# A decode kernel (attention, output projection and gated MLP): TensorE's program in two loops of two rounds, and wide matmuls for half of the output weights

## The chip, the cores and the metric

The kernel runs on one core of one Trainium2 chip. The time is device microseconds from the start of the execution to its end, lower is better. The time line of the profile is some 1.7 us shorter, because it runs from the first instruction to the last.

## The reference, cut to what matters

```python
# x: (4, 1, 512).  32 query heads, 8 heads in the cache, head size 128, all bfloat16
# k_cache, v_cache: (4, 8, 4096, 128); only the last W = 1024 rows count
xn = layernorm(x)
q = xn @ wq                                  # wq: 512 x 4096
p = softmax(q @ k.T * 128 ** -0.5)           # k, v: last 1024 rows, each head for 4 query heads
s = (p @ v) @ wo                             # wo: 4096 x 512
h = gelu(layernorm(xn) @ w1 + b1)            # w1: 512 x 1792
g = silu(h @ w2 + b2)                        # w2: 1792 x 512
return x + s * g
```

With four rows of x there is little arithmetic; nearly all of the work is to read 8 MB of K, 8 MB of V, 4 MB each of wq and wo, and 1.75 MB each of w1 and w2.

## The kernel before

Every operation is recorded in a list for its engine, with the operations that it depends on, and the program is then written out in full. The SyncE queue issues the large loads in a fixed order. The parts that matter here (cuts are marked); PV(g) multiplies the softmax weights of head g by its rows of V:

```python
def load_k(g):                 # 1 MB a head; eight buffers of 1 MB, V takes those of K
    d_k[g] = pg.dma("sp", "k%d" % g, lambda e: e.dma_start(
        kv_buf[:, g, :, :].rearrange("p c d -> p (c d)"), cache_rows(A_k_cache, g)))
# ...
d_wq = [load_wq(0)]
load_k(0)
load_k(1)
d_wq.append(load_wq(1))
for g in range(2, HKV):
    load_k(g)
# ... transposes T(n) and scores S(n): 32 units of 8 tiles, written out
for n in range(LAG, NUN + LAG):
    if n < NUN:
        T(n)
    S(n - LAG)
load_v(0); ...w1...; load_v(1); ...w2...
for g in range(HKV):
    if g >= 2:
        load_v(g)
    if g == 4:                 # 128 rows of wo, scattered over few DMA engines
        R3 = (7 * 512 + 384) * D
        d_wox = [pg.dma("sp", "wox%d" % h, lambda e, h=h: e.dma_start(
            wox_sb[32 * h:32 * h + 12, 0:5, :].rearrange("p j o -> p (j o)"),
            bass.AP(A_wo.tensor, R3 + 60 * h * D, [[5 * D, 3], [15 * D, 4], [1, 5 * D]])),
            t_q) for h in range(2)]
        d_wox.append(...)      # the last 8 rows
    PV(g)
    # ... epilogue of the head before; mlp1 after head 0, mlp2 and mlp3 after head 1
# ...
def wo(tiles, *deps):          # the narrow form: weights are loaded, 4 columns stream
    def fn(pe):
        for w, o, st, sp in tiles:
            for c in range(4):
                last = pe.matmul(psM[:, PS_W + c * 4:PS_W + (c + 1) * 4],
                                 w[:, c * 128:(c + 1) * 128], o,
                                 start=(st and c == 0), stop=sp, skip_group_check=True)
        return last
    return add("pe", fn, *deps)

rows = to_rows()               # after head 7: attention output to rows, as wo is laid out
wo([...scattered rows: 24 matmuls...], rows[2], mlp["g"], *d_wox)
for g0, g1, i0, i1, d in d_wo:         # pieces of wo: 2 + 2 + 2 + 1 heads
    wo([(wo_sb[:, g, i, :], OW[:, i, g * 4:(g + 1) * 4], False, False)
        for g in range(g0, g1) for i in range(i0, i1)], d, rows[0], mlp["g"])
for i0, i1, d in d_w3:                 # last head: 256 rows, then 128
    t_w = wo([(wo_sb[:, 7, i, :], OW3[:, i * 4:(i + 1) * 4], False, i == 2)
              for i in range(i0, i1)], d, rows[1])
# multiply by g, transpose, add x, store
```

The narrow form of wo has the output's 512 columns in four pieces on the partitions of PSUM, and so ends in the layout that the last multiplication wants.

The softmax here doesn't subtract the row's maximum and nothing guards it: scores larger than these inputs give would overflow.

## Time and profile before

| kernel before | value |
|---|---|
| time, median of three runs | 76.72 us (76.69 to 76.80) |
| span in the profile | 75.0 us |
| bytes read | 28.85 MB |
| TensorE instructions written, by the prediction's count | 2204 (1089 matmuls with their weight loads; the trace has 2202 records) |
| last landing of wo (semaphore records) | 71.89 us |
| end of the last wo matmul | 72.2 us |

The page counts 16 DMA engines for the core, and a load of 128 KB or more has 16 landing records on its semaphore (the last piece of wo in before: 70.25 to 71.89 us). Each is taken here as one engine delivering its share. The kernel's waits are for the last of them.

The prediction below shows the page's slices, the chain of waits and the time line. In a group the columns are line, engine, operation, output and inputs, shapes (the weights' rows and columns with a star, then what streams), count, then busy time in us and mean ns of one, then the idle time before and what ended most of it.

```profile
DMA 39%; PE 34%; SPq 15%; DVE 5%; issue 3%
...
L555 PE MATMUL psM<-OW,wo_sb 128*128 128x4 bf16 x124 | 4.1, 167 | 0.8 <-DMA wo_sb<-in_A_wo_dram 0.8
...
L555 PEld LDWEIGHTS psM<-OW,wo_sb 128*128 128x128 bf16 x124 | 3.7, 105 | 1.1 <-DMA wo_sb<-in_A_wo_dram 0.9
```

The narrow matmuls of wo wait 0.8 us for wo's loads. Records overlap: 64 of these matmuls took 1.87 us in the time line, 0.029 us for each, though one record is 167 ns long. So what a group costs is read from the time line, not from its mean.

### The profile page before, as it was taken

Reading aid. Unit: us, or ns where it says so; the run is one execution under the profiler, and the core shown is the slowest. Engines: PE = TensorE matmul, PEld = TensorE weight load, DVE = VectorE, ACT = ScalarE, POOL = GpSimd, SP = SyncE. Lnnn points to the kernel's source line nnn. Section 1 sums busy time; section 2 is a strip of 40 time slices with the busy share of each in tenths; the row PEclk is TensorE's granted clock in tenths of the full one; section 3 lists DMA queues with packets and bytes.
Section 4 is the critical chain, followed back from the end, with each engine's and each line's share of the span. In section 5 each row is a group of like instructions: output and inputs, shape, how many; then the busy total and the mean of one; then the engine's idle time right before and its main releaser. Section 6 shows DMA issues by size and latency. Waiting matters only on the chain.

```text
span 75.0 us, 2384 instructions
## 1 busy us (share of the span) xinstructions
PE 49.1 (66%) x1089; PEld 40.3 (54%) x1089; DVE 41.2 (55%) x84; ACT 9.7 (13%) x16; POOL 7.2 (10%) x19
## 2 busy tenths in 40 slices
PE   0000029965689999959979937910899977379670
PEld 0000029953279989959979902500886555268640
DVE  0778106894258989959977060269639774620020
ACT  0611000000270320303203600230000000000000
POOL 6999300000000000000000000000000000000000
PEclk9999999999999999999999995555555555555555
DMA  1999999998999999999999999999999999999800
GB/s 37 271 413 420 417 420 476 437 420 376 433 437 433 415 433 420 424 415 464 419 398 425 461 413 401 424 420 428 419 429 428 420 409 420 417 411 419 322 25 2
DMA packets 4266, 28.99 MB, mean 387 GB/s; under 512 B 508, under 2 KB 648, under 8 KB 1697
## 3 DMA queue, kind: packets, MB, share of 16 engines
q1 hardware_dynamic: 4206, 28.84, 92.6%
q8 instruction: 8, 0.13, 0.6%
q10 hardware_dynamic: 50, 0.01, 0.1%
q14 instruction: 2, 0.01, 0.0%
HBM read 28.85 MB, written 0.00 MB: 385 GB/s over the span
## 4 chain that ended last, share of the span: by engine, by line
DMA 39%; PE 34%; SPq 15%; DVE 5%; issue 3%
DMA wo_sb<-in_A_wo_dram 26%; PE psK L299 20%; SPq L510 14%; DMA kv_buf<-in_A_k_cache_dram 13%; PE psS L318 6%; DVE kt_buf L305 4%; PE psO L383 3%; PE psS L314 2%; PE psM L555 2%; DVE q_sb L389 1%; PE psK L395 1%; PE psK L367 1%; PE psS L576 1%; SPq L218 1%; SPq L211 0%
## 5 line engine op out<-in xcount | busy, mean ns | idle before, releaser
L299 PE MATMUL psK<-ident,kv_buf 128*128 128x128 bf16 x256 | 20.5, 231 | 11.9 <-DMA kv_buf<-in_A_k_cache_dram 10.7
L305 DVE COPY kt_buf<-psK 128x1024 bf16<-128x1024 bf16 x32 | 21.1, 691 | 7.4 <-PE psK L299 7.3
L299 PEld LDWEIGHTS psK<-ident,kv_buf 128*128 128x128 bf16 x256 | 16.3, 104 | 11.3 <-DMA kv_buf<-in_A_k_cache_dram 10.7
L318 PEld LDWEIGHTS psS<-qT,kt_buf 128*128 128x128 bf16 x256 | 9.4, 96 | 2.1 <-issue 1.2
L318 PE MATMUL psS<-qT,kt_buf 128*128 128x16 bf16 x256 | 10.4, 169 | 0.2 <-issue 0.2
L336 PEld LDWEIGHTS psO<-P_buf,kv_buf 128*128 128x128 bf16 x256 | 7.5, 103 | 3.4 <-DMA kv_buf<-in_A_v_cache_dram 1.8
L336 PE MATMUL psO<-P_buf,kv_buf 128*128 128x16 bf16 x256 | 8.0, 174 | 0.9 <-DVE den_sb L349 0.7
L349 DVE TENSOR_REDUCE den_sb<-psS 128x16 f32<-128x512 f32 x8 | 5.5, 687 | 5.1 <-PE psS L342 4.9
L326 ACT ACTIVATE P_buf<-psS 128x512 bf16<-128x512 f32 x8 | 4.8, 597 | 16.2 <-PE psS L318 16.2
L555 PE MATMUL psM<-OW,wo_sb 128*128 128x4 bf16 x124 | 4.1, 167 | 0.8 <-DMA wo_sb<-in_A_wo_dram 0.8
L342 PE MATMUL psS<-P_buf,ones_bf 128*128 128x512 bf16 x8 | 4.5, 561 | 0.0
L555 PEld LDWEIGHTS psM<-OW,wo_sb 128*128 128x128 bf16 x124 | 3.7, 105 | 1.1 <-DMA wo_sb<-in_A_wo_dram 0.9
L572 DVE TENSOR_TENSOR sg_sb<-psM,g_sb 128x16 f32<-128x16 f32 x1 | 0.2, 185 | 5.8 <-PE psM L555 5.8
L421 PE MATMUL psK<-w_sb,yT 128*32 128x448 bf16 x16 | 2.0, 561 | 1.8 <-issue 1.8
L314 PE MATMUL psS<-negm,ind 128*128 128x512 bf16 x8 | 3.0, 380 | 0.0
L449 PE MATMUL psM<-ident,b_sb 4*128 4x16 bf16 x1 | 0.2, 190 | 3.8 <-DVE hT L444 3.8
L431 DVE SCALAR_TENSOR_TENSOR kt_buf<-kt_buf,psK 128x448 f32<-128x448 f32 x1 | 0.6, 622 | 3.7 <-ACT kt_buf L430 3.7
L449 PEld LDWEIGHTS psM<-ident,b_sb 4*128 4x128 bf16 x1 | 0.1, 99 | 4.3 <-DVE hT L444 4.3
L390 ACT ACTIVATE q_sb<-psO 128x512 bf16<-128x512 f32 x1 | 0.6, 597 | 13.1 <-PE psO L383 13.1
L267 DVE CAST P_buf<-x_bf 4x512 f32<-4x512 bf16 x1 | 1.0, 956 | 2.2 <-DMA x_bf<-in_A_x_dram 2.2
L352 DVE RECIPROCAL rden<-den_sb 128x16 f32<-128x16 f32 x8 | 2.0, 253 | 0.3
L440 DVE TENSOR_TENSOR kt_buf<-kt_buf,psK 128x448 bf16<-128x448 f32 x1 | 2.1, 2083 | 0.0
(74 smaller groups left out, 36.0 us busy)
## 6 DMA issues: line engine op xcount, KB each, us to landing
kv_buf<-in_A_k_cache_dram SPq DMA_DIRECT2D x8, 1024.0 KB, 20.6
kv_buf<-in_A_v_cache_dram SPq DMA_DIRECT2D x8, 1024.0 KB, 24.0
wq_sb<-in_A_wq_dram SPq DMA_DIRECT2D x2, 2048.0 KB, 11.4
w_sb<-in_B_w_dram SPq DMA_DIRECT2D x2, 1792.0 KB, 28.3
wo_sb<-in_A_wo_dram SPq DMA_DIRECT2D x3, 1024.0 KB, 24.0
wo_sb<-in_A_wo_dram SPq DMA_DIRECT2D x1, 512.0 KB, 19.6
wo_sb<-in_A_wo_dram SPq DMA_DIRECT2D x1, 256.0 KB, 16.4
wo_sb<-in_A_wo_dram SPq DMA_DIRECT2D x1, 128.0 KB, 14.6
```

The lines of the kernel that those rows point to most:

```text
L299: last = pe.transpose(psK[n % NB][:, j * 128:(j + 1) * 128], kv_buf[:, g, u * UT + j, :], ident[:, :])
L305: cp[n] = add("dve", lambda e: e.tensor_copy(kt_buf[:, n % NKT, :], psK[n % NB][:, 0:1024]), t, sc.get(n - NKT))
L314: pe.matmul(psS[g % 2][:, 0:512], ind[:, :], negm[:, :], start=True, stop=False, skip_group_check=True)
L318: last = pe.matmul(psS[g % 2][:, c * 16:(c + 1) * 16], kt_buf[:, n % NKT, j * 128:(j + 1) * 128], qT[:, g * 16:(g + 1) * 16], start=False, ...
L326: ex[g] = add("act", lambda e: e.activation(P_buf[:, g, :], psS[g % 2][:, 0:512], AF.Exp, scale=SCALE), sc[n])
L336: last = pe.matmul(pso[:, 0:16], kv_buf[:, (HKV + g) % NS, c, :], P_buf[:, g, c * 16:(c + 1) * 16], start=(c == 0), stop=(c == NC - 1))
L342: den[g] = add("pe", lambda pe: pe.matmul(psS[g % 2][:, 0:512], ones_bf[:, :], P_buf[:, g, :], start=True, stop=True), ex[HKV - 2 + g % 2] ...
L349: v = add("dve", lambda e: e.tensor_reduce(den_sb[:, cs], bass.AP(psS[g % 2], 0, [[512, 128], [1, 16], [16, NC]]), AX.X, ALU.add), den[g])
L383: last = pe.matmul(psO[m // 4][32 * s:32 * s + 32, 0:512], xT[:, c, :], wq_sb[:, c, m * 512:(m + 1) * 512], start=(c == 0), stop=(c == 3), ...
L440: v = add("dve", lambda e: e.tensor_tensor(bass.AP(kt_buf, 4 * UT * 128, [[NKT * UT * 128, 128], [1, 32], [32, FC]]), f32k(3).rearrange("p ...
L510: d_wo.append((g0, g1, i0, i1, pg.dma("sp", "wo%d" % n, lambda e: e.dma_start(wo_sb[:, g0:g1, i0:i1, :], wo_r[:, g0:g1, i0:i1, :]))))
L555: last = pe.matmul(psM[:, PS_W + c * 4:PS_W + (c + 1) * 4], w[:, c * 128:(c + 1) * 128], o, start=(st and c == 0), stop=sp, skip_group_che ...
```

## The change

The intent, as I read it from the code and the profile before: a shorter TensorE program needs fewer instruction fetches (eight packets of 16 KB in before), after each of which in before about one more DMA engine was late; the scattered rows of wo go to fewer engines (3, 3 and 8 for before's three loads, 5 and 3 for the two after); and half of wo goes through the wide form (4 to 32 columns of weights, 512 columns streaming), a quarter as many matmuls. The wide form leaves partial sums in four groups of partitions, so the kernel has ScalarE copy them out of PSUM and follows with a *fold*: four matmuls against a 0/1 matrix, which add the groups and bring the result into the narrow form's layout. The copy and the fold are fp32. The second MLP layer is done in the same way, between V heads 3 and 4. Smaller differences are left out of the cut below, among them four copies on ScalarE of the softmax weights for V's second round.

```diff
+                with pe.Fori(0, 2, 1) as i:          # one loop for K, one for V, two rounds each
+                    ...
+                        with pe.If(i < 1):           # second MLP layer, in V's first round only
 # ...
+    fold = sb([128, 4], F32)
 # ...  K: four buffers, used twice; V: four buffers, used twice
-            kv_buf[:, g, :, :].rearrange("p c d -> p (c d)"), cache_rows(A_k_cache, g)),
-            )
+            kv_buf[:, g % NG, :, :].rearrange("p c d -> p (c d)"), cache_rows(A_k_cache, g)),
+            t_last[g - NG] if g >= NG else None, sem=d_k[g - NG].sem if g >= NG else None)
 # ...
-    d_wq = [load_wq(0)]
-    load_k(0)
-    load_k(1)
-    d_wq.append(load_wq(1))
-    for g in range(2, HKV):
+    d_wq = [load_wq(0), load_wq(1)]
+    for g in range(NG):
         load_k(g)
 # ...  scattered rows: 80 rows on five engines, 48 on three
+        bass.AP(A_wo.tensor, R3 + b0 * D, [[4 * D, n], [4 * n * D, 4], [1, 4 * D]])),
+        t_q) for p0, n, b0 in ((0, 5, 0), (32, 3, 80))]
 # ...
+    def folded(pe, src, o, first, last):
+        for c in range(4):
+            r = pe.matmul(psM[:, o + c * 4:o + (c + 1) * 4], src[:, c * 128:(c + 1) * 128],
+                          fold[:, :], start=first and c == 0, stop=last, skip_group_check=True)
+        return r
 # ...  the tail
+    def wide(tiles, *deps):
+        def fn(pe):
+            last = None
+            for i, o, w, st, sp in tiles:
+                m = o.shape[1]
+                last = pe.matmul(psK[2][32 * i:32 * i + m, 0:1024].bitcast(F32), o, w,
+                                 start=st, stop=sp, tile_position=(0, 32 * i))
+            return last
+        return add("pe", fn, *deps)
-    wo([...scattered rows, 24 narrow...], rows[2], mlp["g"], *d_wox)
-    for g0, g1, i0, i1, d in d_wo:
+    for g0, g1, i0, i1, d in d_wo[:2]:
+        t_w = wide([... 8 of them ...], d, rows[0])
+        if g0 == 0:
+            wide([... 4 of the scattered rows ...], rows[2], *d_wox)
+    w_c = add("act", lambda e: e.activation(f32r(6), psK[2][:, 0:1024].bitcast(F32), AF.Copy),
+              t_w)
+    add("pe", lambda pe: folded(pe, f32r(6), PS_W, True, False), w_c, c_fold, mlp["g"])
+    for g0, g1, i0, i1, d in d_wo[2:]:
         wo([(wo_sb[:, g, i, :], OW[:, i, g * 4:(g + 1) * 4], False, False)
             for g in range(g0, g1) for i in range(i0, i1)], d, rows[0], mlp["g"])
```

## The prediction

> **What bounds the kernel now.** I read the page first, then the chain of waits, then the waits, then the time line of the last 35 us, and last the packet and semaphore records of the trace itself.
>
> The page's slices: the transfers fill the kernel from its third to its seventieth microsecond.
>
> ```profile
> PE   0000029965689999959979937910899977379670
> PEclk9999999999999999999999995555555555555555
> DMA  1999999998999999999999999999999999999800
> ...
> q8 instruction: 8, 0.13, 0.6%
> ...
> HBM read 28.85 MB, written 0.00 MB: 385 GB/s over the span
> ```
>
> The DMA row is at nine or more tenths from slice 1 to slice 36, so the kernel streams 28.85 MB and everything else must fit under that. The inconspicuous line is the instruction queue: eight packets, 0.13 MB, so 16 KB each. TensorE's clock falls to half at 45 us and stays there.
>
> The chain of waits, by time (start us, length us, what), ends so:
>
> ```profile
> 51.30 19.64 DMA wo_sb<-in_A_wo_dram
> 70.93 0.05 issue
> 70.98 0.59 PE psM L555 x16
> 71.57 0.04 issue
> 71.61 0.61 PE psM L555 x12
> 72.24 0.20 DVE sg_sb L572
> ```
>
> TensorE waits for wo, does 28 small matmuls as the last pieces land, and a fixed tail follows (multiply, transpose, add, store). Before 40 us the chain runs through TensorE, but only because it fed buffers early enough. The end is set by the last landing of wo.
>
> The semaphore records say when that is. The last piece of wo (128 KB) lands on 16 DMA engines: five at 70.25 to 70.57 us, one at 71.05, ten at 71.53 to 71.89. So the slow engines are 1.3 to 1.5 us behind. Following the landings back: until 22.9 us all 16 are within 0.5 us. The eight instruction packets start at 24.30, 30.78, 36.82, 43.05, 49.17, 57.72, 64.89 and 70.11 us, and the group of late engines grows by about one after each (one 8 KB instruction packet at 39.93 makes the one that is 0.5 us late); none ever catches up. Three more fall back by 1.5 us when the scattered piece of wo (128 rows) has been issued: 2 x 20 KB + 1 KB on each of three engines at 64 KB per 2.45 us is 41 / 26.1 = 1.57 us. So 3 + 7 + 1 late, 5 punctual.
>
> The same fetches stop TensorE. In the time line:
>
> ```profile
> 43.31 0.36 PE L421 MATMUL psK<-w_sb,yT 128*32 128x448 bf16 x1
> ...
> 45.48 1.68 PE L421 MATMUL psK<-w_sb,yT 128*32 128x448 bf16 x15 [1.81 <-issue]
> ```
>
> A wait on nothing the profile knows, over 2.4 us after the fetch at 43.05. The holes before matmuls 222, 349, 476 and 603 all end 2.3 to 2.4 us after a fetch began. Counting the program's instructions (two per matmul), these are 256 apart, at places 452, 708, 964 and 1220; 452 + 7 x 256 = 2244 is past the program's 2204, so eight fetches, as seen.
>
> [...]
>
> **The change, part by part.**
>
> 1. Loops. The program for TensorE shrinks from 2204 to 1234 instructions (1089 to 593 matmuls written; those in loops run twice). The same block boundaries then give fetches at 452, 708, 964 and 1220: four in place of eight, if a block stays held for the second round. What it is worth on the transfers: nothing per engine hit, since one late engine is enough to hold the last landing 1.3 to 1.5 us back. Four fewer late engines only lower the maximum within their spread, up to 0.2 us. TensorE's holes before 50 us lie under the transfers: 0.
>
> 2. Scattered piece of wo: k = 5 and k = 3, 16 KB per engine. Engines 0 to 2 carry 32 KB, 3 and 4 carry 16 KB: 32 / 26.1 = 1.23 us and 0.61 us late in place of 1.57. It counts only if no fetched engine is later: 0 to -0.3 us.
>
> 3. Order of loads. Both wq first, K heads 4 to 7 into the buffers of 0 to 3. From the landings of before (2 MB by 8.2, then 2.45 us a MB) wq is complete at 13.1, K0 at 15.6, and the queue holds work to 27.2 us. K4 is issued when K0 is transposed, about 17.4 us. V4 is issued after PV of head 0, about 46 us, and is due at about 51. No starvation: 0 us, with 5 us or more in hand.
>
> 4. The K part ends at about 42.5 (16 units at 0.69 us of VectorE copy from 31 us), as before (42.3). The second MLP layer waits for w2 (51 to 52.6) and the 4.4 us chain on VectorE; it is 14 wide matmuls (14 x 0.12 = 1.7 us at half clock, from the 15 of line 421 in 1.68), a copy (0.6) and four small fp32 matmuls (about 0.5), so the second V round starts near 56 us, against V7 at 62.2. Slack about 1.4 us; a 2.3 us fetch in the middle of it (place 964 is there) would eat it and leave up to 0.45 us.
>
> 5. The tail. Before: from 66.51 us, 24 + 64 narrow matmuls in 0.88 + 1.87 = 2.75 us, free at 69.2, half a microsecond before wo's third piece lands:
>
> ```profile
> 66.51 0.88 PE L555 MATMUL psM<-OWx,wq_sb 44*128 44x4 bf16 x24 [0.53 <-DVE OWx L547]
> 67.33 1.87 PE L555 MATMUL psM<-OW,wo_sb 128*128 128x4 bf16 x64
> 69.73 1.01 PE L555 MATMUL psM<-OW,wo_sb 128*128 128x4 bf16 x32 [0.54 <-DMA wo_sb<-in_A_wo_dram]
> ```
>
> After: 20 wide ones at about 0.12 us, 2.4 us from 66.35[...]: 69.0; the ScalarE copy out of PSUM 0.65: 69.7; the fold 0.6: 70.3. Then 32 narrow (1.0), 16 (0.5) and 12 (0.4): 72.2. It was 72.2. So the wide form uses up the slack and sets the end jointly with the transfers: 0 to +0.4 us.
>
> Sum: parts 1 and 2 together -0.1 to -0.4, part 4 0 to +0.4, part 5 0 to +0.4. The middle is about 0. I shade it down, because three estimates in parts 4 and 5 are on the careful side (half clock, no overlap of fold and copy), and because both changes to the load pattern can only lower the latest landing: -0.3 us, 76.4.
>
> **The rivals.**
>
> a) [...]no fetch happens at all. [...] Against it: then the last rows of wo would best be spread on all engines, and the author did not. Effect: the latest engines are 0 to 2 at +1.23, the last landing near 71.6, all of V 0.3 us earlier: 76.3 or a little less.
>
> b) [...]the loop over K (places 108 to 638, three blocks) and the one over V refetch in the second round, ten or more fetches, some on engines already hit. For it: [...]that no fetch was ahead of need. Effect: engines 3 us late, 1.5 us later: 78.2.
>
> c) TensorE becomes the bound in the tail: the clock stays at half, fold and copy longer than estimated, or a fetch hole after V: 77.0 to 77.5.
>
> d) Load starvation where K4 or V4 waits for a buffer: a hole in the DMA row. Against it the slack of part 3. It would cost a microsecond or more.
>
> **Range and chances.** With four fetches 76.1 to 77.0; a) 76.0 to 76.5; b), c), d) 77 to 78.5. I take 76.4, 75.5 to 77.4 for 8 in 10. Faster by over 2% needs under 75.2, which asks for the latest engine to be 1.5 us earlier, that is no lateness at all: 0.09. Slower by over 2% needs above 78.25, rival b) or d): 0.07. Within 2%: 0.84.
>
> **What would show it.** The instruction queue's packets: four says part 1, none says a), ten says b). The landings of the last wo piece: a latest one at 71.5 to 71.9 says that lateness is set by any fetched engine; 70.6 would refute it. In the waits, wo matmuls on line 685 waiting for wo's DMA says transfers bind; waiting for the ScalarE copy says c). The DMA row must stay at nine from slice 1 to 36. The prediction is wrong if the stream ends a microsecond earlier or later, or if the second V round starts after 58 us.

Cuts in the text are marked: they are statements about the hardware that did not come from this case's runs, with what hung on them, and one term of part 5. Without that term the steps no longer add up to its 69.0 us; the sums stand as they were put on record, 72.2 us for the tail and 76.4 us for the time. k is the number of DMA engines that a load lands on: apart from one early record each, the two 60 KB loads of before have three landings each (53.91 to 54.03 and 54.67 to 54.87 us), the scattered loads of the changed kernel five and three (51.21 to 52.37 and 51.84 to 52.07 us). The holes: in before TensorE's matmuls stood idle for 0.16, 0.81, 0.42 and 1.81 us, until 2.3 to 2.4 us after each of the first four fetches began. The 0.6 us of the fold, and the 0.5 us in part 4, were estimates, with no row given for them; each fold was measured at 1.87 us.

## The result, and the profile after

| | before | after |
|---|---|---|
| time, median of four runs each, alternating | 76.76 us (76.69 to 77.06) | 77.78 us (77.67 to 77.88) |
| span in the profile | 75.0 us | 76.1 us |
| mean granted clock of TensorE | 0.802 | 0.804 |
| last landing of wo | 71.89 us | 71.89 us |

The ratio is 1.0125, with a 95% interval of 1.0092 to 1.0157: the changed kernel is slower, by less than 2%. A ratio here is the mean time of one kernel's fast runs over the mean of the other's fast runs of the same rounds, so not quite the ratio of the medians quoted.

The page of the changed kernel, its slices, its instruction queue and the chain's shares:

```profile
PE   0000741879999993599999959892879956496970
...
DMA  1999999999999999999999999989999999999200
...
q8 instruction: 5, 0.08, 0.4%
...
PE 12%; DVE 3%; ACT 1%; issue 1%
```

The DMA row ends as before: the stream of data is no later. The instruction queue has five packets in place of eight. In the chain's shares DMA is gone, where it had 39% before. Part of that is the view: these shares sum to 17%, because the chain starts only at 62.34 us, at the sequencer's wait for the last head of V, and is not followed back to that head's landing at 62.25. So V's loads still decide when the tail starts; what the chain shows is that no load of wo is on it. The chain itself (start us, length us, what):

```profile
62.54 1.00 PE psO L438 x32
...
66.63 2.54 PE psK L698 x19
69.16 0.02 issue
69.19 0.61 ACT kt_buf L711
69.79 0.04 issue
69.84 1.87 PE psM L573 x8
71.70 1.61 PE psM L685 x60
73.32 0.02 issue
73.34 0.20 DVE sg_sb L722
```

After the last head's PV (line 438) and its epilogue, the end waits for compute alone: wide matmuls (698), the copy on ScalarE (711), the fold (573), then all 60 narrow matmuls of the rest (685) one behind the other with no wait for wo. The last landing is at 71.89, when the narrow matmuls have just begun, and they end at 73.32, 1.1 us later than before. The surprise is the fold: four matmuls took 1.87 us, as long as 64 narrow ones. The groups by shape say what they are:

```profile
L573 PE MATMUL psM<-fold,kt_buf 128*128 128x4 f32 x16 | 3.7, 357 | 0.7 <-ACT kt_buf L711 0.7
L573 PEld LDWEIGHTS psM<-fold,kt_buf 128*128 128x128 f32 x16 | 3.6, 328 | 1.6 <-ACT kt_buf L711 1.6
...
L685 PEld LDWEIGHTS psM<-OW,wo_sb 128*128 128x128 bf16 x60 | 1.9, 107 | 0.0
```

Four matmuls are written for each of the two folds, and the group counts 16: each fp32 matmul is recorded as two (called passes below), each with its own load of a 128 x 128 fp32 weight tile. One load is recorded at 328 ns against 107 for bfloat16, and the records overlap less than in bfloat16: eight passes in 1.87 us are 0.23 us each (0.21 from start to start), 60 narrow bfloat16 matmuls in 1.61 us are 0.027 each. Why the fp32 load takes three times as long is not shown by any run here.

The landings of the last piece of wo, worked out from the semaphore records of the trace (its 16 increments, one for each DMA engine):

| kernel | punctual engines | between | late engines | last landing |
|---|---|---|---|---|
| before | 5, at 70.25 to 70.57 | 1, at 71.05 | 10, at 71.53 to 71.89 | 71.89 us |
| after | 7, at 70.18 to 70.33 | 1, at 70.79 | 8, at 71.37 to 71.89 | 71.89 us |

Two engines fewer are late, and the last landing is where it was.

### The profile page after: what moved, and what is told of

Its sections match the earlier page's. It is cut to its first block, busy times and chain, and to the rows that moved or that the text cites. A ratio compares the mean times of both kernels' runs of the same rounds, so it can differ in the third digit from the quotient of the medians.

```text
span 76.1 us, 2251 instructions
## 1 busy us (share of the span) xinstructions
PE 53.3 (70%) x993; PEld 41.1 (54%) x993; DVE 40.7 (54%) x85; ACT 13.1 (17%) x22; POOL 7.9 (10%) x24
## 5 line engine op out<-in xcount | busy, mean ns | idle before, releaser
L419 PE MATMUL psS<-qR,kt_buf 128*128 128x16 bf16 x256 | 10.7, 170 | 0.0
L419 PEld LDWEIGHTS psS<-qR,kt_buf 128*128 128x128 bf16 x256 | 9.8, 97 | 1.3 <-issue 0.3
L487 PE MATMUL psO<-wq_sb,xT 128*32 128x512 bf16 x32 | 3.8, 628 | 2.9 <-DMA wq_sb<-in_A_wq_dram 2.6
L573 PEld LDWEIGHTS psM<-fold,kt_buf 128*128 128x128 f32 x16 | 3.6, 328 | 1.6 <-ACT kt_buf L711 1.6
L573 PE MATMUL psM<-fold,kt_buf 128*128 128x4 f32 x16 | 3.7, 357 | 0.7 <-ACT kt_buf L711 0.7
L493 DVE CAST q_sb<-psO 128x512 bf16<-128x512 f32 x1 | 0.7, 692 | 6.4 <-PE psO L487 6.4
L487 PEld LDWEIGHTS psO<-wq_sb,xT 128*32 128x32 bf16 x32 | 0.9, 129 | 4.9 <-DMA wq_sb<-in_A_wq_dram 3.5
L564 PE MATMUL psK<-w_sb,hT 128*4 128x512 bf16 (+1 forms) x14 | 1.9, 626 | 1.5 <-DVE hT L553 1.5
L449 ACT ACTIVATE P_buf<-P_buf 128x512 bf16<-128x512 bf16 x4 | 2.4, 621 | 1.6 <-PE psS L445 1.6
L711 ACT ACTIVATE kt_buf<-psK 128x512 f32<-128x512 f32 x1 | 0.6, 597 | 11.4 <-PE psK L698 11.4
```

The costliest lines, as they stand in the source:

```text
L419: last = pe.matmul(psS[lg % 2][:, c * 16:(c + 1) * 16], kt_buf[:, n % NKT, j * 128:(j + 1) * 128], qR[:, lg * 16:(lg + 1) * 16], start=Fal ...
L449: pc[lg] = add("act", lambda e: e.activation(P_buf[:, lg, :], P_buf[:, NG + lg, :], AF.Copy), den[g], cls="pc")
L487: last = pe.matmul(psO[m // 4][32 * s:32 * s + 32, 0:512], xT[:, c, :], wq_sb[:, c, m * 512:(m + 1) * 512], start=(c == 0), stop=(c == 3), ...
L573: r = pe.matmul(psM[:, o + c * 4:o + (c + 1) * 4], src[:, c * 128:(c + 1) * 128], fold[:, :], start=first and c == 0, stop=last, skip_grou ...
```

## The experiments

My theory (A) after the comparison: the whole loss is the fp32 fold on TensorE, and with a cheap fold the loads would set the end again. The rivals: (B) the loss comes from the loops, their waits or their fetches, and the tail only shows it; (C) the wide form and the copy out of PSUM are too long as such, whatever the fold costs.

### 1. The fold in bfloat16

The copy writes bfloat16 and the 0/1 matrix is bfloat16; nothing else changes.

```diff
+    fold16 = sb([128, 4], BF16)
+    c_f16 = add("gp", lambda e: e.tensor_copy(fold16[:, :], fold[:, :]), c_fold)
-    def folded(pe, src, o, first, last):
+    def folded(pe, src, o, first, last, f=fold):
-                          fold[:, :], start=first and c == 0, ...
+                          f[:, :], start=first and c == 0, ...
-    w_c = add("act", lambda e: e.activation(f32r(6), psK[2]..., AF.Copy), t_w)
-    add("pe", lambda pe: folded(pe, f32r(6), PS_W, True, False), w_c, c_fold, mlp["g"])
+    w_c = add("act", lambda e: e.activation(kt_buf[:, 6, 0:512], psK[2]..., AF.Copy), t_w)
+    add("pe", lambda pe: folded(pe, kt_buf[:, 6, 0:512], PS_W, True, False, fold16),
+        w_c, c_f16, mlp["g"])
```

> The changed kernel with one thing undone: the copy out of PSUM writes bf16 and the wo fold runs in bf16 (a small loss of accuracy), so 4 single matmuls in place of 8 fp32 passes. Theory A (the fp32 fold is 1.87 us of TensorE between the wide matmuls and the last 60 narrow ones, and it alone makes TensorE later than the landings): fold about 0.2 us, TensorE free at 70.1, then bound by the last landing at 71.9 again: 76.7 us, ratio to before 1.000 +- 0.003. Rival B (the loops, their branches and fetches, and the late second half of V): no change, 77.6 or more. Rival C (wide matmuls at half clock): the wide stretch of 2.54 us stays and so does most of the loss: above 77.3.

Measured: 76.65 us (six runs, 76.50 to 76.79) against 76.70, ratio 0.9984 [0.9968, 1.0000]. The groups by shape of this kernel, with the tail's fold alone:

```profile
L575 PE MATMUL psM<-fold,kt_buf 128*128 128x4 bf16 x4 | 0.3, 172 | 0.7 <-ACT kt_buf L713 0.7
L575 PEld LDWEIGHTS psM<-fold,kt_buf 128*128 128x128 bf16 x4 | 0.2, 109 | 1.6 <-ACT kt_buf L713 1.6
```

Four written matmuls are now four passes. In its time line the fold begins as late as in the changed kernel, but is 0.27 us long:

```profile
69.93 0.27 PE L575 MATMUL psM<-fold,kt_buf 128*128 128x4 bf16 x4 [0.70 <-ACT kt_buf L713]
70.06 2.23 PE L687 MATMUL psM<-OW,wo_sb 128*128 128x4 bf16 x60
```

The 60 narrow matmuls take 2.23 us instead of 1.74, because they now wait for wo's landings, and in the chain the DMA is back (16.64 us of it, ending at 71.64). The whole loss has gone with one data type, while loops, wide form and copy stayed. B and C fall as the main cause.

### 2. The tail all narrow, the rest as changed

```diff
-    for g0, g1, i0, i1, d in d_wo[:2]:
-        ... wide ...
-    w_c = ...; add("pe", ... folded ...)
-    for g0, g1, i0, i1, d in d_wo[2:]:
+    wo([(wox_sb[:, a, :], OWx[:, a * 4:(a + 1) * 4], a == 0, False) for a in range(4)],
+       rows[2], mlp["g"], *d_wox)
+    for g0, g1, i0, i1, d in d_wo:
```

> The changed kernel with its tail undone: all seven whole wo groups and the scattered rows by narrow matmuls, no copy, no fold; loops, order of loads and k=5/k=3 kept. Theory A: 80 narrow matmuls of about 31 ns from 66.6, free at 69.2, wo's third piece waits for its DMA, end bound by the landing: 76.7 us, ratio 1.000 +- 0.003, the same as the bf16 fold. Rival B: 77.5 or more. Rival C predicts 76.7 too but then the bf16 fold must stay above 77.3.

Measured: 76.67 us (six runs), ratio 0.9988 [0.9971, 1.0004]. Its time line waits for wo again, twice, as before did:

```profile
69.56 1.02 PE L685 MATMUL psM<-OW,wo_sb 128*128 128x4 bf16 x32 [0.70 <-DMA wo_sb<-in_A_wo_dram]
70.81 1.27 PE L685 MATMUL psM<-OW,wo_sb 128*128 128x4 bf16 x28 [0.23 <-DMA wo_sb<-in_A_wo_dram]
```

So everything in the change but the tail is worth nothing measurable, neither gain nor loss, although fetches, loops, load order and the middle all changed. And the narrow tail had 0.93 us of waiting in it: there was no need for a shorter one.

### 3. The kernel before with the new tail

The wide tail, the copy and the fp32 fold put into the kernel before, with its unrolled program, its load order and its scattered rows (six wide matmuls in its layout).

```diff
 # in the kernel before
+    for g0, g1, i0, i1, d in d_wo[:2]:
+        t_w = wide([... as in the change ...], d, rows[0])
+        if g0 == 0:
+            wide([(a % 4, OWx[:, a * 4:(a + 1) * 4], wox_sb[:, a, :], False, False)
+                  for a in range(5)]
+                 + [(1, OWx[0:8, 20:24], wox_sb[0:8, 5, :], False, False)], rows[2], *d_wox)
+    w_c = add("act", ... AF.Copy), t_w)
+    add("pe", lambda pe: folded(pe, f32r(6), PS_W, True, False), w_c, c_fold, mlp["g"])
```

> The kernel before with only the wide tail added: wide matmuls for four wo groups and the scattered rows, copy, fp32 fold; no loops. Theory A: 22 wide matmuls, copy 0.6, fold 1.87, then 60 narrow: about +1.1 us, 77.8 us, ratio 1.014. Rival B: at most +0.3, 77.0.

Measured: 78.61 us (four runs), ratio 1.0238 [1.0220, 1.0257]. The end of its chain:

```profile
66.89 3.48 PE psK L586 x19
70.39 0.61 ACT kt_buf L600
71.04 1.87 PE psM L575 x8
72.91 1.61 PE psM L564 x60
```

The size was a miss: 0.8 us more than expected. The time line shows why: the scattered rows in this layout took 1.52 us in six wide matmuls, against 0.59 us in four, so the wide part is 3.48 us and not 2.54. The direction stands, and more strongly: the tail alone, in a program with no loop, makes the kernel slower. The fold is 1.87 us here too.

### 4. The loops written out

The changed kernel, with the two rounds written out and a semaphore of its own for every load.

```diff
-            t_last[g - NG] if g >= NG else None, sem=d_k[g - NG].sem if g >= NG else None)
+            t_last[g - NG] if g >= NG else None)
 # the same for V
-            pg.emit_pe(pe)
+            pg.emit("pe", pe)      # after the first values of the semaphores have been set
```

> The changed kernel with TensorE's two loops written out (same order of work, 985 matmuls, about 2000 instructions), nothing else. Theory A: seven or eight 16 KB instruction fetches in place of five, last landing still at 71.8 to 71.9, tail unchanged: 77.7 us, same as the changed kernel within 0.2. Rival B (branches and refetches cost time): 0.5 us or more faster, 77.2 or less. If fewer fetches had helped: slower than 78.0.

Measured: 77.52 us (four runs), ratio 1.0110 [1.0088, 1.0133], with eight instruction packets. The loss stays without the loops. The median is 0.26 us under that of the changed kernel, a little more than the 0.2 expected; the two intervals overlap, so the times alone do not establish that. The time lines show a difference, though. The last head's PV in the changed kernel:

```profile
62.54 1.00 PE L438 MATMUL psO<-P_buf,kv_buf 128*128 128x16 bf16 x32 [0.91 <-PEq L101]
```

and unrolled:

```profile
62.16 1.02 PE L438 MATMUL psO<-P_buf,kv_buf 128*128 128x16 bf16 x32 [0.98 <-DMA kv_buf<-in_A_v_cache_dram]
```

The data it needs had landed at 62.25 in the first and at 62.12 in the second (semaphore records). In the loop the matmuls start 0.29 us after the landing, and what released them is TensorE's sequencer (line 101 is the one that waits and then lowers the reused semaphore); unrolled it is 0.04 us. The same 0.29 to 0.30 us stands before this PV in all ten traces with loops, and 0.04 to 0.05 in the kernel before (both its traces) and here. So this wait costs about 0.25 us in the loops; whether by the reused semaphore or by the loop around it was not separated, since this run undoes both. That is the part of rival B that holds. With a cheap fold it is hidden: experiment 1 has it too.

### 5. The fold twice

```diff
+    add("pe", lambda pe: folded(pe, f32r(6), 256, True, True), w_c, c_fold, mlp["g"])
     add("pe", lambda pe: folded(pe, f32r(6), PS_W, True, False), w_c, c_fold, mlp["g"])
```

> The changed kernel with the fp32 wo fold done twice (the first into unused PSUM columns, not used after). Theory A (the fold lies on the path that sets the end, nothing hides it): one more 1.87 us: 79.6 us, ratio 1.038. If part of the fold overlapped something, less: 78.7 or below.

Measured: 79.59 us (four runs) against 76.90, ratio 1.0349 [1.0331, 1.0367]. Its chain:

```profile
69.88 3.57 PE psM L573 x16
73.45 1.61 PE psM L685 x60
```

Eight more passes add 1.70 us to the fold, and the kernel's time rises by about as much (1.81 by the medians). The fold is on the path in full.

### 6. and 7. The same four matmuls alone

How much of the 1.87 us is the halved clock? Four fp32 matmuls with 128 columns of weights and 4 streaming were added to the kernel of experiment 1, away from the tail. First near 17 us:

```diff
+    def f_alone(pe):
+        for c in range(4):
+            last = pe.matmul(psM[:, 256 + c * 4:260 + c * 4], ident32[:, :], ident32[:, 0:4],
+                             start=(c == 0), stop=True, skip_group_check=True)
+        return last
+    add("pe", f_alone, c_id32)
```

> The bf16-fold version with four fp32 matmuls of the fold's shape (128x128 weights, 4 columns) run once more by themselves near 17 us, where TensorE still has its full clock; result unused. Theory A with the clock as part of it: 8 passes of 0.11 to 0.15 us, about 1 us, where the tail's at half clock took 0.23 each. If the fp32 weight load costs the same at any clock: 1.9 us again. The time stays near 76.7 in both cases, because the first half has slack.

Measured: they took 1.81 us there (one look, 77.51 us, state unknown; one DMA engine was 0.7 us later than usual, so the time is not used). That seemed to say that the clock doesn't matter, but the expectation had the clock wrong: eight bfloat16 transposes just before them took 1.04 us, and 0.61 us for the like later at full clock, so TensorE was slow at that point, by the times of its matmuls. The page's clock row reads 9 there only because the trace's first clock record begins at 22.15 us; before a record the row is filled with full speed. Then the same matmuls right behind the K loop, where the granted clock is 1.00:

> The bf16-fold version with the four fp32 matmuls run once by themselves right after the K loop, near 44 us, in the middle of a stretch in which TensorE's other matmuls show full speed (8 transposes in 0.61 us). If the half clock doubled the fold: 8 passes in about 0.95 us here. If not: 1.8 us. The time stays at 76.7 within 0.3, since that stretch has slack.

Measured (one look, 76.54 us): the time line at that point, and below it two rows of the table of stretches, the first of this run, the second of the changed kernel at its fold; the seventh figure after the stretch itself, counts in brackets aside, is the granted clock (PEclk), 1.00 and 0.50:

```profile
43.13 1.05 PE L618 MATMUL psM<-ident 128*128 128x4 f32 x8 [0.34 <-issue]
```

```profile
43.10:44.10 1.00, 0.97 (x8) 0.97 (x8) 0.00 (x0) 0.32 (x1) 0.00 (x0) 1.00 0.97 410
69.80:71.70 1.90, 1.86 (x14) 1.86 (x15) 0.00 (x0) 0.00 (x0) 0.00 (x0) 0.50 0.46 174
```

At clock 1.00 eight passes take 1.05 us, 0.13 each; in the tail, at 0.50, 1.87 us, 0.23 each. From start to start the passes are 0.11 us apart here and 0.21 in the tail; near 17 us they were 0.21 apart too. The half clock nearly doubles the fold. Even at full clock it would have been above the 0.6 us of the prediction.

### 8. The fold at another place

Theory A has two forms: TensorE is occupied for 1.87 us, or it idles until the copy is there. The fold was moved behind the 32 narrow matmuls of wo's third piece, where the copy is already done (at 69.71 us; the fold starts at 70.56).

```diff
-    add("pe", lambda pe: folded(pe, f32r(6), PS_W, True, False), w_c, c_fold, mlp["g"])
     for g0, g1, i0, i1, d in d_wo[2:]:
-            ... False, False)
+            ... g == GW and i == 0, False)
+        if g0 == GW:
+            add("pe", lambda pe: folded(pe, f32r(6), PS_W, False, False), w_c, c_fold)
```

> The changed kernel with the fp32 fold put behind the 32 matmuls of wo's third piece, so that the copy out of PSUM (0.6 us) lies under them. Theory A in its full form (it is TensorE's own occupation that counts, not the wait for the copy): wo's third piece from 69.6 to 70.7, fold to 72.5, the last 28 matmuls to 73.4: 77.7 us, as the changed kernel within 0.2. If the copy's latency was most of the loss: 0.6 us faster, 77.1.

Measured: 77.64 us (four runs) against 76.75, ratio 1.0116 [1.0099, 1.0132]. Its chain:

```profile
51.11 18.52 DMA wo_sb<-in_A_wo_dram
69.68 1.02 PE psM L685 x32
70.70 1.71 PE psM L573 x8
72.41 0.76 PE psM L685 x28
```

The chain begins with wo's third landing at 69.6, so the wait for the copy is off it, and the fold's own 1.71 us behind it make the kernel as slow as the changed one. It is the occupation of TensorE.

### 9. and 10. Which DMA engines are late

Fifteen small loads of 1 to 15 rows with 512 bytes each, issued behind the last weights, to tell from their landings which of the engines are the late ones: in the kernel of experiment 1 and in the kernel before.

```diff
+    d_probe = [pg.dma("sp", "pr%d" % k, lambda e, k=k: e.dma_start(
+        wq_sb[0:k, 1, 256 * k - 256:256 * k], bass.AP(A_wo.tensor, 0, [[D, k], [1, 256]])), t_q)
+        for k in range(1, 16)]
```

> The bf16-fold version with 15 tiny loads of k = 1 to 15 partitions (512 B each) behind the last weights, to tell which of the 16 DMA engines are late at the end: [...]the list of landings of load k has one entry more than that of k - 1, and its place says how late engine k - 1 is. Expected: engines 0 to 2 late by 1.0 to 1.3 us (32 KB), one of 3 and 4 late by about 0.6 and the other by more (8 KB instruction packet), four of 5 to 15 late by 1.4 to 1.6 (one for each instruction packet before 60 us), seven punctual. Time unchanged, 76.7 within 0.3.

Measured: 76.73 us, one look. Engine k - 1 stands for the landing that the load of k rows has beyond those of the load of k - 1. Read off the landings, late are engines 0, 1 and 2 (32 KB of the scattered rows), 3 (16 KB and a small instruction packet), and 5, 6, 9 and 14, which had a fetch; 4 is about 0.6 us late with its 16 KB; 7, 8 and 10 to 13 are punctual (engine 15 is touched by none of these loads; by count it is punctual). So, by these landings, the scattered rows went to the engines of the smallest probes, as the prediction's numbers 0 to 4 had it, and engines with a fetch and engines with the extra rows end at the same lateness (in the changed kernel's trace all eight late ones lie within 71.37 to 71.89 us, the punctual ones at 70.18 to 70.33).

> The kernel before with the same 15 tiny loads behind its last weights. Expected: engines 0 to 2 late by 1.5 us (41 KB), seven of the others late by 1.3 to 1.6 (instruction packets), one by about 0.6, five punctual. Time unchanged, 76.7 within 0.3.

Measured: 77.43 us, one look, state unknown, 0.7 us slower than expected. Three engines, 0 to 2 with the scattered rows, landed last at 72.07, 72.23 and 72.59, where the trace without probes ended at 71.89. Late were 0 to 2, 5, 6, 9 and 11 to 14, with 3 in between; punctual 4, 7, 8 and 10, and by count 15. That is the ten late and one between seen without probes; why three were later still is open, and with one look it can't be told from chance.

### 11. The last head's rows spread evenly

The kernel of experiment 1 with all 512 rows of wo's last head on all 16 engines, and nothing scattered (which also spares TensorE 13 matmuls).

```diff
-    d_wox = [ ... five and three engines ... ]
-    d_w3 = [ ... 384 rows ... ]
+    for n, (i0, i1) in enumerate(((0, 2), (2, 3), (3, 4))):
+        load_wo(4 + n, 7, 8, i0, i1)
```

> The bf16-fold version, but the last head's 128 scattered rows loaded like all others, 8 KB on each of the 16 engines, none on k=5 and k=3. If the latest instruction-fetched engine sets the last landing, every engine gets 8 KB more, 8 / 26.1 = 0.31 us, and the fetched ones stay 1.5 us late: last landing 72.2, time 77.0, ratio to before 1.004. If the engines with 32 KB set it: faster, 76.3 or less.

Measured: 77.00 us (six runs) against 76.85, ratio 1.0017 [1.0004, 1.0030], as expected. Eleven engines land at 70.50 to 70.89, one at 71.39 and four at 71.94 to 72.11. Here only the engines with a fetch are late, by the usual 1.3 us or so, and they now carry their share of all of the rows: the last landing is 0.14 us later than in experiment 1. By the ratios (1.0017 over 0.9984, of 76.7 us, from two batches on different chips) the scattered rows are worth about a quarter of a microsecond against the even spread.

### 12. A third of the last rows through GpSimd's queue

Engines 10 to 13 are punctual in experiment 9. The last 128 of the 384 rows were sent through GpSimd's queue, meant for these four; that they would land there was a guess, which no earlier run had tested.

```diff
-    d_w3 = [ ... for i0, i1 in ((0, 2), (2, 3))]
+    d_pads = [gp_pad("g0", 10, 0)]            # ten small rows first
+    d_gq = pg.dma("gp", "g1", lambda e: e.dma_start(
+        wo_sb[:, 7, 2, :], bass.AP(A_wo.tensor, (7 * 512 + 2) * D,
+                                   [[3 * 32 * D, 4], [3 * D, 32], [1, D]])))
+    d_w3 = [ ... for i0, i1 in ((0, 2),)] + [(2, 3, d_gq)]
```

> An attempt to beat both: the bf16-fold version with the last head's last 128 of 384 rows (128 KB) loaded from GpSimd's queue[...]. If it lands there: every engine is spared 8 KB, 0.31 us, engines 10 to 13 get 32 KB, 1.2 us, last landing near 71.6, 76.4 us, ratio 0.995. If GpSimd's loads go to other engines (the late ones, or all 16): 76.7 to 78.0.

Measured: 77.04 us (six runs), ratio 1.0023 [1.0010, 1.0036]. It failed: the pattern of late engines stayed, and the V and wo pieces on all 16 were some 0.2 us later, with a last landing of 72.03. The load seems to have been spread over all engines; that is inferred from the landings, and why is open.

## Why the prediction was wrong, point by point

The time predicted was 76.4 us in a range of 75.5 to 77.4, and 77.78 was measured, outside it. "Within 2%" held.

**Part 1, loops: right on the transfers, wrong in the count.** The last landing is 71.89 in both kernels, as the step said: one late engine is enough. The fetches are five, not four. The prediction's own count would have given it: before crosses seven boundaries (452 to 1988) and has eight packets, one more than it crosses; after crosses four, so five. I counted that extra packet for before and left it out for after. The other programs fit the count: the unrolled one, of 2002 instructions, has seven boundaries and eight packets, and that of experiment 11, which is shorter, four. The counts fit, but the times don't prove it: in the changed kernel the fetches began at 23.01, 29.17, 49.36, 57.04 and 73.18 us, the fourth just as V's second round began. The fifth came after the last landing, so four could make an engine late, as predicted. By the prediction's places the K loop covers three blocks, and its second round ran between 29.4 and 44.5 us without a 16 KB packet, so rival b (a refetch in the second round) is refuted, and rival a (no fetch) as well.

**Part 2, scattered rows: within its range, at its zero end.** Expected 0 to -0.3 us against the scatter of before; the last landing did not move. Experiment 11 makes another comparison, with an even spread.

**Part 3, load order: right.** The DMA row stays at eight or nine tenths to the end of the stream (the prediction read nine throughout in before; one slice there, too, is an eight), and the last V head lands at 62.25, before at 62.22. Rival d did not come.

**Part 4, the middle: the same mis-sized term, without consequence.** The second V round was to start near 56 us and started at 57.42, most of it because the MLP's fold took 1.87 us in place of 0.5 as well. The slack before the last V head swallowed it: experiment 2 still has that fold and is as fast as before.

**Part 5, the tail: this step failed, in the term "the fold 0.6".** The terms, as the prediction put them, against the trace:

| step | predicted end | measured end |
|---|---|---|
| wide matmuls | 69.0 | 69.16 |
| copy out of PSUM | 69.7 | 69.80 |
| fold | 70.3 | 71.70 |
| last narrow matmul | 72.2 | 73.32 |

Until the fold all is within 0.2 us. The fold was 1.87 us in place of 0.6, 1.27 more, and the kernel is 1.02 us slower by the medians. The rest of the difference is that the narrow matmuls took 1.61 us instead of the 1.9 predicted. The mechanism was half named ("uses up the slack and sets the end jointly"): TensorE does set the end, but not jointly, since no matmul of line 685 waited for a landing. The wait for ScalarE's copy, the sign that the prediction gave for rival c, is there, before the fold (0.7 us). Rival c said that TensorE might become the bound with a longer fold, at 77.0 to 77.5; it came a little beyond that upper end. The size was wrong because nothing in the profile of before carried it: no fp32 matmul with 128 columns of weights is in it, only the final transpose with 16, at 0.38 us, and the text gives no working for its 0.6. A pass costs 0.23 us, two passes a matmul, at the half clock that the prediction itself had read for the tail.

**The shading down.** The sum's middle was "about 0" and I took 0.3 off, with the reason that the estimates were careful. The one that mattered was four times too low in the MLP's fold and three times in the tail's. A term with no row to rest on should have widened the range upwards; instead it was counted as careful.

**What stays open.** Which block each of the fetches brought, whether GpSimd's load was spread and why, and what made three engines later in experiment 10. No version beats the kernel before beyond the noise: experiments 1 and 2 are ties with it (0.9984 and 0.9988), both bound by the same last landing.

## What to carry to other kernels

Before trading many small matmuls for few large ones plus a clean-up, take each term of the clean-up from a row of the same data type, shape and clock; if there is none, measure it alone. Here four fp32 matmuls cost as much as 64 bfloat16 ones, and writing the copy in bfloat16, a small loss of accuracy with the result still correct, gave all of it back. And first look at how long the shorter work could be used at all: TensorE was waiting for loads in that tail, and the loads' end stayed at 71.89 us with eight late DMA engines in place of ten, so neither fewer matmuls nor fewer late engines gained anything.
